# Attention, MLP and routed experts on one core: column-group gate, a new hand-written order, one looped overflow body

## The chip, the core and the metric

The kernel runs on one core of one Trainium2 chip. The metric is device time in microseconds (us): the median of several executions of the whole program. Engines are named as in the profile: PE is the matrix engine (PEld is its loading of weights), DVE the vector engine, ACT the scalar engine, POOL the general engine, SP the engine that issues most DMAs.

## The reference, cut to what matters

```python
# attention: 4 batches x 8 heads, 576 tokens, head_dim 64; heads 0-3 a window of 32 keys,
# heads 4-7 every 4th of the last 128 keys
scores = where(mask, q @ k.T / 8, -1e9)
x = softmax(scores) @ v                      # -> x of 2304 tokens x 512
# block MLP
h = x @ w_in                                 # 512 -> 2048
x = (h * cos(h)) @ w_out                     # 2048 -> 512
# router and experts: 8 experts, two per token
logits = x @ w_gate
noisy = logits + log1p(exp(x @ w_noise)) * noise
top2, their softmax weights
out[t] += weight * (relu(x[t] @ w1[e]) @ w2[e])   # 512 -> 1024 -> 512, for both experts e of t
```

## The kernel before

Three stages follow one another on PE and overlap on the other engines. **Attention** runs in 16 units `u`, each a pair of heads: `a_loadqk` and `a_loadv` (DMA), `a_scores` (PE), `a_exp` (DVE maximum L489, ACT exponentials L509 in many small instructions), `a_norm` (DVE sum and reciprocal, tile `sm`, L520 and L521), and `a_part(u, 0..2)`: transposes (`mt`, L534) and products with the values (`mo`, L554), copied out to `xraw`. `x_split(blk, c)` (L594 on ACT, L595 on DVE) turns `xraw` into the high and low parts `xhl` of the next stage.

**The MLP** runs over 6 blocks of 384 tokens, each in 16 steps `f` of 128 hidden columns, 96 steps in all. In a step PE does `g1` (L607, 12 matmuls into `ph`) and, two steps behind, `g2` (L632, 9 matmuls into `acc`). `post` turns `ph` into `g`: ACT L614, DVE `r` L615, ACT sine and square L617 and L618, DVE `r` again L619, ACT L622, POOL L623. Block 0's 16 steps also bring in the weights: eight pairs `j`, each in four parts `k`. `w_load(j, k)` and for pair 7 `w_piece(7, 0..7)` (half as wide) are DMAs; `w_bits` is three DVE operations (L332, L333, L334, tiles `bits` and `cut`); `w_parts` is an ACT copy (L340) and a POOL subtraction (L341) that leave the two halves in `wm`. Later blocks find all weights in place.

**The router** follows each block: `r_rows` (scaled rows `x1`, written out), `r_trans` (PE transposes `mx` L667, DVE copy `x1t` L668), `r_gate` (fp32 matmuls `mg` L675 against `wgn`, the 8 gate and 8 noise columns; DVE copy `lg` L678, `az` L681), `r_exp`, `r_top`, `r_top2`, `r_pick`, `r_rank`, `r_send`. They are done beside steps of the next block; the last block's router (`LAST`) stands among the first expert's matmuls. **The experts** (`pe` L888, `ye` L923, scatter L936) fill the second half, for up to CAP = 608 tokens of an expert. An overflow test (L1087 to L1093) and `tc.If(over > CAP)` (L1095) stand at the end; with this input no expert exceeds CAP, so its body, eight loops with code of their own, is jumped over.

The order is written by hand. Each engine runs its instructions in the order in which the program calls the functions, and waits at its own head only. `OPENING` is the sequence before and around the first step (`Q4` = `a_loadqk(4)`, `W01` = `w_load(0, 1)`, `B10` = `w_bits(1, 0)`, `P` = `w_parts`, `S`, `E`, `N`, `T`, `A` = the parts of attention, `X` = `x_split`, `G` = pieces of `g1`). `BESIDE` has lines `step:place names`: what is called beside that step, at place -1 before its `g1`, at 0, 1, 2 after pieces of `g2`; for example `8:1 a_loadqk(7) w_bits(5,1) w_parts(5,0) a_exp(6) a_norm(6) w_parts(5,1) w_piece(7,0) w_bits(5,2)`. The DMAs of SP share 8 semaphores, so at most 8 are under way and an issue that has to wait holds all later ones.

Of the kernel before, what the change touches and what calls it, by code (L numbers as in the profile page):

```python
# [102 lines left out]
13:2 w_bits(7,4) w_parts(7,4) w_piece(7,7) w_bits(7,5) w_parts(7,5)
14:0 a_part(7,1)
14:1 w_bits(7,6) w_parts(7,6)
14:2 w_bits(7,7) a_part(7,2) w_parts(7,7)
15:-1 x_split(1,2)
15:0 x_split(1,3)
16:0 a_loadv(8)
# [1069 lines left out]
```

## Time and profile before

| | |
|---|---|
| median of 3 runs | 1045.11 us (1044.08 to 1047.26) |
| the profiled execution's own time | 1044.4 us |
| its span, first to last instruction | 1042.7 us |
| mean granted PE clock over the span | 0.976 |
| PE, PEld, DVE, ACT, POOL busy | 994.9, 878.4, 513.4, 472.4, 353.9 us |
| chain that ended last, by engine | PE 68%, DVE 13%, ACT 8%, POOL 3% |

The granted clock is PE's own, as a share of its full 2.4 GHz; 0.50 is the level of 1.2 GHz. Busy shares are averages over the whole span. The table of stretches (busy time of each engine, granted clock, in each) shows where PE is not busy; the timeline of one engine shows in square brackets how long it was idle ahead of an instruction and which instruction let it go; the chain of waits follows the work that ended last back from step to step, so its times are those that count.

### The profile page before, as it was taken

The page shows a single profiled execution, that of the slowest core. Times are in us where ns is not written, and L with a number is a line of the kernel's source. Part 1 is how long each engine was busy: PE and PEld are TensorE (multiplying, and loading weights), DVE is VectorE, ACT ScalarE, POOL GpSimd, SP SyncE. Part 2 cuts the span into 40 slices and gives each one's busy share as a digit, 9 for nine tenths or more (in the row PEclk, how much of TensorE's full clock was granted, in tenths as well). Part 3 has the DMA queues.
Part 4 walks back from the last instruction along what each step waited for, and adds up shares of the span by engine and source line. Part 5 has one row for each costly group of instructions (what it writes and reads, how often), then busy time and mean ns, then how long its engine had stood idle before and what let it go on. Part 6 is the DMA issues. An engine that isn't in the chain of part 4 may idle for free.

```text
span 1042.7 us, 15952 instructions
## 1 busy us (share of the span) xinstructions
PE 994.9 (95%) x6047; PEld 878.4 (84%) x6047; DVE 513.4 (49%) x1096; ACT 472.4 (45%) x1019; POOL 353.9 (34%) x495
## 2 busy tenths in 40 slices
PE   9788899999999999999999989999999999999995
PEld 7677778888888889989988888899898979898984
DVE  7777755535644453453566444554453535353321
ACT  7677665545656555455465223333241414242210
POOL 5455533343253342142153221441313232322211
PEclk9798889999999999999999999999999999999998
DMA  9972032233221100000324324653434244441201
GB/s 241 349 243 80 21 76 66 90 89 90 79 51 40 48 1 1 31 1 1 112 74 135 122 43 151 225 168 118 149 123 151 72 160 135 155 148 51 69 21 51
DMA packets 71334, 105.13 MB, mean 101 GB/s; under 512 B 31475, under 2 KB 45043, under 8 KB 71248
## 3 DMA queue, kind: packets, MB, share of 16 engines
q1 hardware_dynamic: 61264, 76.34, 23.3%
q0 software_dynamic: 9984, 27.68, 8.6%
q8 instruction: 49, 0.80, 0.4%
q14 instruction: 37, 0.30, 0.1%
HBM read 85.42 MB, written 19.59 MB: 101 GB/s over the span
## 4 chain that ended last, share of the span: by engine, by line
PE 68%; DVE 13%; ACT 8%; issue 4%; POOL 3%; DMA 2%; SPq 1%; DVEq 0%; ACTq 0%; POOLq 0%
PE ye L923 21%; PE pe L888 20%; PE ph L607 11%; PE acc L632 9%; PE mgx L872 2%; DVE r L615 1%; DVE bits L333 1%; DVE bits L332 1%; PE mg L675 1%; ACT r L617 1%; DVE r L619 1%; ACT r L618 1%; PE sc L476 1%; POOL tab L760 1%; DVE cut L334 1%
## 5 line engine op out<-in xcount | busy, mean ns | idle before, releaser
L607 PE MATMUL ph<-xhl,wm 128*128 128x384 f32 x1152 | 230.6, 349 | 8.2 <-DVE r L619 4.3
L632 PE MATMUL acc<-wm,g 128*128 128x512 f32 x864 | 230.9, 405 | 5.8 <-POOL g L623 3.3
L923 PE MATMUL ye<-we,h 128*128 128x512 f32 (+1 forms) x960 | 230.0, 396 | 0.0
L607 PEld LDWEIGHTS ph<-xhl,wm 128*128 128x128 f32 x1152 | 209.8, 195 | 17.6 <-DVE r L619 5.9
L923 PEld LDWEIGHTS ye<-we,h 128*128 128x128 f32 (+1 forms) x960 | 172.9, 183 | 43.0
L632 PEld LDWEIGHTS acc<-wm,g 128*128 128x128 f32 x864 | 161.2, 192 | 35.7 <-POOL g L623 5.6
L623 POOL TENSOR_TENSOR g<-r,g 128x384 fp32r<-128x384 f32 x96 | 97.1, 1013 | 220.1 <-ACT g L622 219.5
L888 PE MATMUL pe<-xga,we 128*128 128x352 f32 x768 | 128.2, 326 | 1.0 <-ACT xga L874 0.6
L888 PEld LDWEIGHTS pe<-xga,we 128*128 128x128 f32 x768 | 125.0, 188 | 1.7 <-ACT xga L874 0.8
L890 ACT ACTIVATE h<-pe 128x352 fp32r<-128x352 f32 (+1 forms) x128 | 54.2, 424 | 131.2 <-PE pe L888 131.2
L891 DVE SCALAR_TENSOR_TENSOR h<-pe,h 128x352 fp32r<-128x352 f32 (+1 forms) x128 | 60.7, 475 | 98.4 <-ACT h L890 97.7
L936 POOL DMA_INDIRECT out<-old,tir x35 | 35.2, 1007 | 211.8 <-DVE old L934 206.7
L615 DVE SCALAR_TENSOR_TENSOR r<-r,ph 128x384 f32<-128x384 int32 x96 | 53.0, 552 | 104.5 <-ACT r L614 104.5
L802 DVE TENSOR_TENSOR we<-wraw,we 128x512 fp32r<-128x512 f32 x128 | 93.0, 734 | 11.0 <-ACT we L801 7.9
L888 PE MATMUL pe<-xgb,we 128*128 128x256 f32 x768 | 94.1, 284 | 3.0 <-DVE xgb L875 1.5
L888 PEld LDWEIGHTS pe<-xgb,we 128*128 128x128 f32 x768 | 93.0, 192 | 3.8 <-ACT xgb L874 1.9
L619 DVE SCALAR_TENSOR_TENSOR r<-r,ph 128x384 f32<-128x384 f32 x96 | 52.8, 550 | 84.5 <-ACT r L618 84.5
L934 DVE SCALAR_TENSOR_TENSOR old<-ye,wts,old 128x512 f32<-128x512 f32 (+1 forms) x35 | 26.3, 750 | 133.4 <-PE ye L923 133.4
L622 ACT ACTIVATE g<-r 128x384 fp32r<-128x384 f32 x96 | 50.2, 523 | 68.5 <-DVE r L619 55.0
L801 ACT ACTIVATE we<-wraw 128x512 fp32r<-128x512 f32 x128 | 78.6, 623 | 0.0
L617 ACT ACTIVATE r<-r 128x384 f32<-128x384 f32 x96 | 50.2, 523 | 55.9 <-DVE r L615 55.5
L614 ACT ACTIVATE r<-ph 128x384 int32<-128x384 f32 x96 | 46.6, 486 | 58.2 <-PE ph L607 51.6
(175 smaller groups left out, 993.1 us busy)
## 6 DMA issues: line engine op xcount, KB each, us to landing
wraw<-in_we SPq DMA_DIRECT2D x64, 512.0 KB, 5.8
raw<-in_wm SPq DMA_DIRECT2D x28, 512.0 KB, 9.3
vts<-in_v SPq DMA_DIRECT2D x13, 384.0 KB, 4.2
x1d<-x SPq DMA_DIRECT2D x18, 256.0 KB, 2.4
out<-zt SPq DMA_DIRECT2D x18, 256.0 KB, 3.7
...
```

Of the source, the lines that this page charges most:

```text
L607: nc.tensor.matmul(ph, w[:, a, o:o + P], XHL[blk, c][:, x, :], start=(c == 0 and n == 0), stop=(c == 3 and n == 2))
L615: nc.vector.scalar_tensor_tensor(r, n, -TWO_PI, ph, op0=ALU.mult, op1=ALU.add)
L617: nc.scalar.activation(r, r, AF.Sin, scale=0.5)
L619: nc.vector.scalar_tensor_tensor(r, r, 0.5, ph, op0=ALU.subtract, op1=ALU.mult)
L623: nc.gpsimd.tensor_tensor(g[:, 1, :], r, g[:, 0, :].bitcast(F32), op=ALU.subtract)
L632: nc.tensor.matmul(ACC[blk][t], g[:, a, t * P:(t + 1) * P], w[:, x, 1024 + j * DM:1024 + (j + 1) * DM], start=(f == 0 and n == 0), stop=(f ...
L801: nc.scalar.activation(t[:, 0, fs], raw, AF.Copy)
L802: eng.tensor_tensor(t[:, 1, fs], raw, t[:, 0, fs].bitcast(F32), op=ALU.subtract)
L888: nc.tensor.matmul(ph[:, :n], w[:, a, o:o + P], x[:, b, c, :], start=(c == 0 and i == 0), stop=(c == 3 and i == 2))
L890: nc.scalar.activation(h[:, 0, f, :], ph[:, :n], AF.Relu)
L891: nc.vector.scalar_tensor_tensor(h[:, 1, f, :], ph[:, :n], 0.0, h[:, 0, f, :].bitcast(F32), op0=ALU.max, op1=ALU.subtract)
L923: nc.tensor.matmul(acc, h[:, a, f, o:o + n], w[:, b, (f % 4) * DM:(f % 4 + 1) * DM], start=(f == 0 and i == 0), stop=(f == 7 and i == 2))
```

## The change

**Gate.** `wgn` becomes 128x4x32, of which a DMA fills 16 columns each and POOL zeroes the rest. In `r_gate` the sides of the matmul are swapped: `wgn[:, c]` (32 columns) is loaded as weights, the 128 tokens of `x1t` stream, and the four chunks `c` of the contraction go to four groups of 32 output partitions of one bank. One DVE copy takes all 384 columns to `lp`. A new function `r_logits` transposes `lp` in three pieces on PE (`ml`), and one DVE reduction adds the four groups into `lg`; `az` follows as before. `r_logits` stands at `20:0`, `36:0`, `52:0`, `68:0`, `84:0`, after the first `acc` of the step behind the gate's, and for `LAST` after `m_g1(0, 0, 2)`, with `r_exp` behind it.

**Order.** `OPENING` and the lines of `BESIDE` for steps 0 to 16 are rewritten. `w_parts` is split in `w_hi` (ACT) and `w_lo` (POOL), `a_part` in `a_tr` (transposes) and `a_o` (products), and these pieces stand apart. What each computes stays.

**Overflow.** The eight loops become one body inside two nested loops; its branch is the same, `over > CAP`. The test has one DVE operation fewer.

```diff
 OPENING = (
-    "S0 S1 E0 N0 Q4 E1 W01 S2 W02 T00 T01 N1 E2 S3 T02 T10a N2 A00 T11 A01 W10 E3 W11 T12 T20a A10a T21a "
-    "A11a N3 B00 T22a X0p A20a W03 B01 T30a V4 P00 A21a X1 T32a W20 X2p S4 P01 T31a G00 "
-    "B10 G10 W23 G11 W12 W21 E4 B11 A30a A31a X3 P10 P11 G01 G02 G12 W13 W22"
+    "W01 S0 S1 W02 E0 N0 S2 W03 E1 T00 Q4 T01 T02 E2 N1 N2 S3 T10a A00 W10 E3 T11 T12 A01 T21a T20a T22a "
+    "A10a N3 B00 A11a B01 W20 W23 X1 T31a A20a P00 X0p P01 T32a A21a T30a S4 G10 G11 W11 E4 W12 B10 W13 "
+    "X2p A30a A31a B11 X3 W22 P10 P11 G00 G01 V4 G12 W21 G02"
 )
 BESIDE = """
-4:1 w_parts(3,0) w_load(4,3) a_scores(5)
-4:2 w_bits(3,1)
-5:-1 a_exp(5) w_parts(3,1) w_load(5,0) a_norm(5) w_load(5,1) w_bits(3,2)
+4:0 a_scores(5) w_hi(2,3) w_load(5,0) w_lo(2,3) w_bits(3,0)
+4:1 w_hi(3,0) w_lo(3,0) a_loadv(5)
+4:2 w_bits(3,1) a_loadqk(6)
+5:-1 w_bits(3,2) a_exp(5) w_hi(3,1) w_load(5,1) w_lo(3,1)
+5:0 a_norm(5)
...
-8:1 a_loadqk(7) w_bits(5,1) w_parts(5,0) a_exp(6) a_norm(6) w_parts(5,1) w_piece(7,0) w_bits(5,2)
+8:0 w_hi(4,3) a_loadv(6) a_scores(6) w_lo(4,3) w_bits(5,0)
+8:1 a_exp(6) w_hi(5,0) w_bits(5,1) w_piece(7,2) a_loadqk(7) w_lo(5,0) a_norm(6) w_bits(5,2)
...
-11:1 a_exp(7) w_bits(7,0) w_parts(6,3) w_bits(7,1) w_parts(7,0) w_parts(7,1)
+11:1 w_bits(7,0) w_hi(6,3) a_exp(7) w_hi(7,0) w_lo(6,3) w_lo(7,0) w_bits(7,1) w_hi(7,1) w_lo(7,1)
...
 19:2 r_gate(0) a_loadqk(9)
-20:0 a_norm(8)
+20:0 a_norm(8) r_logits(0)
 20:1 r_exp(0)
...
+    def w_hi(j, k):
+        nc.scalar.activation(WM[j][:, 0, w_fs(j, k)], CUT[j, k].bitcast(F32), AF.Copy)
+
+    def w_lo(j, k):
         fs = w_fs(j, k)
         raw = CUT.pop((j, k)).bitcast(F32)
-        nc.scalar.activation(WM[j][:, 0, fs], raw, AF.Copy)
         nc.gpsimd.tensor_tensor(WM[j][:, 1, fs], raw, WM[j][:, 0, fs].bitcast(F32), op=ALU.subtract)
...
-    wgn = cpool.tile([P, 4, 2 * NE], F32, name="wgn")
+    wgn = cpool.tile([P, 4, 32], F32, name="wgn")
...
+        G.memset(wgn, 0.0)
...
-        nc.sync.dma_start(wgn, wg)
+        nc.sync.dma_start(wgn[:, :, :2 * NE], wg)
...
-                nc.tensor.matmul(mid[:, t * 2 * NE:(t + 1) * 2 * NE], RT[blk][t][:, c, :], wgn[:, c, :],
-                                 start=(c == 0), stop=(c == 3))
-        lg = small.tile([P, NTB, 2 * NE], F32, tag="lg", name=f"lg{blk}")
-        nc.vector.tensor_copy(lg, mid[:, :NTB * 2 * NE].rearrange("p (t e) -> p t e", t=NTB))
+                nc.tensor.matmul(mid[32 * c:32 * c + 32, t * P:(t + 1) * P], wgn[:, c, :], RT[blk][t][:, c, :],
+                                 start=True, stop=True)
+        lp = tpool.tile([P, DM], F32, tag="t2", name=f"lp{blk}")[:, :TB]
+        nc.vector.tensor_copy(lp, mid[:, :TB])
+        RT[blk] = lp
+
+    def r_logits(blk):
+        lp = RT[blk]
+        mid = r_bank(f"ml{blk}", blk)
+        for t in range(NTB):
+            nc.tensor.transpose(mid[:, t * P:(t + 1) * P], lp[:, t * P:(t + 1) * P], ident)
+        lg = small.tile([P, NTB, 32], F32, tag="lg", name=f"lg{blk}")
+        nc.vector.tensor_reduce(lg, mid[:, :TB].rearrange("p (t c e) -> p t e c", c=4, e=32), axis=AX.X, op=ALU.add)
...
     with tc.If(over > CAP):
-        for e in range(NE):
-            nt = nc.values_load(nti[0:1, e:e + 1], min_val=NTILE, max_val=NTILE + -(-(NT - CAP) // P))
-            with tc.For_i(NTILE, nt, 1) as i:
+        nt = nc.values_load(nti[0:1, 1:2], min_val=NTILE, max_val=NTILE + -(-(NT - CAP) // P))
+        with tc.For_i(NTILE, nt, 1) as i:
+            with tc.For_i(0, NE, 1) as e:
```

What the order looks like on the engines, at three places. First SP's queue behind the last DMA of the constants (`tab`), before; `raw0` holds pair 0 of the weights, and `kts` and `qts` belong to unit 4, `vts` too:

```order
L428 DMA tab_81<-padt_191 128x300
L276 DMA kts_83<-in_kT 128x576
L279 DMA qts_85<-in_qT 64x9x64 x2
L307 DMA raw0_104<-in_wm 128x1024 x2
L307 DMA raw1_379<-in_wm 128x1024 x2
L307 DMA raw0_104<-in_wm 128x1024
L284 DMA vts_84<-in_v 64x128
L285 DMA vts_84<-in_v 96x8x128
```

and the same place after:

```order
L445 DMA tab_81<-padt_191 128x300
L317 DMA raw0_104<-in_wm 128x1024 x3
L286 DMA kts_83<-in_kT 128x576
L289 DMA qts_85<-in_qT 64x9x64 x2
L317 DMA raw1_364<-in_wm 128x1024
L317 DMA raw2_453<-in_wm 128x1024 x2
```

The three loads of pair 0 stand ahead of unit 4's keys and queries, and the values of unit 4 further behind.

Second, DVE at steps 12 and 13, before:

```order
L521 RECIPROCAL sm7_1372<-sm7_1372 128x9
L615 SCALAR_TENSOR_TENSOR r0_12_1426<-r0_12_1426,ph0_12_1408 128x384
L332 TENSOR_SCALAR bits7_2_1435<-piece7_2_1280 128x256
L333 SCALAR_TENSOR_TENSOR bits7_2_1435<-piece7_2_1280,bits7_2_1435 128x256
L334 SCALAR_TENSOR_TENSOR cut7_2_1434<-piece7_2_1280,bits7_2_1435 128x256
L332 TENSOR_SCALAR bits7_3_1442<-piece7_3_1432 128x256
L333 SCALAR_TENSOR_TENSOR bits7_3_1442<-piece7_3_1432,bits7_3_1442 128x256
L334 SCALAR_TENSOR_TENSOR cut7_3_1441<-piece7_3_1432,bits7_3_1442 128x256
L619 SCALAR_TENSOR_TENSOR r0_12_1426<-r0_12_1426,ph0_12_1408 128x384
L595 TENSOR_TENSOR xhl1_1_1455<-xraw_82,xhl1_1_1455 128x384
L615 SCALAR_TENSOR_TENSOR r0_13_1484<-r0_13_1484,ph0_13_1469 128x384
L619 SCALAR_TENSOR_TENSOR r0_13_1484<-r0_13_1484,ph0_13_1469 128x384
```

and after:

```order
L342 TENSOR_SCALAR bits7_2_1430<-piece7_2_1161 128x256
L343 SCALAR_TENSOR_TENSOR bits7_2_1430<-piece7_2_1161,bits7_2_1430 128x256
L344 SCALAR_TENSOR_TENSOR cut7_2_1429<-piece7_2_1161,bits7_2_1430 128x256
L628 SCALAR_TENSOR_TENSOR r0_12_1434<-r0_12_1434,ph0_12_1411 128x384
L342 TENSOR_SCALAR bits7_3_1447<-piece7_3_1440 128x256
L343 SCALAR_TENSOR_TENSOR bits7_3_1447<-piece7_3_1440,bits7_3_1447 128x256
L344 SCALAR_TENSOR_TENSOR cut7_3_1446<-piece7_3_1440,bits7_3_1447 128x256
L632 SCALAR_TENSOR_TENSOR r0_12_1434<-r0_12_1434,ph0_12_1411 128x384
L608 TENSOR_TENSOR xhl1_1_1456<-xraw_82,xhl1_1_1456 128x384
L628 SCALAR_TENSOR_TENSOR r0_13_1488<-r0_13_1488,ph0_13_1473 128x384
L342 TENSOR_SCALAR bits7_4_1495<-piece7_4_1051 128x256
L343 SCALAR_TENSOR_TENSOR bits7_4_1495<-piece7_4_1051,bits7_4_1495 128x256
```

One piece of weight work has moved ahead of the first `r` of step 12, and between the two `r` of step 13, where nothing stood, there is one now.

Third, PE at the gate of block 0, beside steps 19 and 20, before:

```order
L632 MATMUL acc1_2_1744<-wm0_436,g1_1_1708 128x512 x3
L675 MATMUL mg0_1833<-wgn_187,x1t0_0_1768 128x16 x4
L675 MATMUL mg0_1833<-wgn_187,x1t0_1_1787 128x16 x4
L675 MATMUL mg0_1833<-wgn_187,x1t0_2_1813 128x16 x4
L607 MATMUL ph1_4_1853<-xhl1_0_1253,wm2_707 128x384 x3
L607 MATMUL ph1_4_1853<-xhl1_1_1455,wm2_707 128x384 x3
L607 MATMUL ph1_4_1853<-xhl1_2_1623,wm2_707 128x384 x3
L607 MATMUL ph1_4_1853<-xhl1_3_1632,wm2_707 128x384 x3
L632 MATMUL acc1_0_1742<-wm1_533,g1_2_1778 128x512 x3
L632 MATMUL acc1_1_1743<-wm1_533,g1_2_1778 128x512 x3
```

and after:

```order
L645 MATMUL acc1_2_1745<-wm0_430,g1_1_1709 128x512 x3
L688 MATMUL mg0_1834<-x1t0_0_1769,wgn_187 32x128 x4
L688 MATMUL mg0_1834<-x1t0_1_1788,wgn_187 32x128 x4
L688 MATMUL mg0_1834<-x1t0_2_1814,wgn_187 32x128 x4
L620 MATMUL ph1_4_1852<-xhl1_0_1257,wm2_692 128x384 x3
L620 MATMUL ph1_4_1852<-xhl1_1_1456,wm2_692 128x384 x3
L620 MATMUL ph1_4_1852<-xhl1_2_1629,wm2_692 128x384 x3
L620 MATMUL ph1_4_1852<-xhl1_3_1633,wm2_692 128x384 x3
L645 MATMUL acc1_0_1743<-wm1_544,g1_2_1779 128x512 x3
L698 MATMUL ml0_1878<-ident_131,lp0_1847 128x128 x3
L645 MATMUL acc1_1_1744<-wm1_544,g1_2_1779 128x512 x3
```

The 12 calls of the gate stand where they stood, with weights and stream swapped, and the three transposes `ml` stand in PE's queue 15 matmuls behind them.

## Rows read from the trace of the kernel before

**Rows 1.** The page: busy time and share; the chain that ended last, by engine

```profile
PE 994.9 (95%) x6047; PEld 878.4 (84%) x6047; DVE 513.4 (49%) x1096; ACT 472.4 (45%) x1019; POOL 353.9 (34%) x495
...
PE 68%; DVE 13%; ACT 8%; issue 4%; POOL 3%; DMA 2%; SPq 1%; DVEq 0%; ACTq 0%; POOLq 0%
```

**Rows 2.** Stretches: length, busy us (instructions) per engine, PE clock, DMA share, GB/s

```profile
26.00:52.00 26.00, 19.30 (x125) 17.39 (x127) 18.44 (x31) 16.03 (x45) 12.30 (x13) 0.74 1.06 349
...
40.00:157.00 117.00, 101.24 (x600) 86.08 (x599) 85.07 (x151) 79.73 (x202) 61.66 (x62) 0.87 0.43 128
157.00:1031.00 874.00, 859.26 (x5117) 763.97 (x5115) 400.26 (x881) 366.51 (x703) 272.18 (x386) 1.00 0.28 90
```

**Rows 3.** Timeline of DVE, opening: start, us, operation, [idle before <- releaser]

```profile
27.29 0.69 DVE L332 TENSOR_SCALAR bits<-raw 128x512 uint32<-128x512 uint32 x1 [3.84 <-DMA raw<-in_wm]
```

**Rows 4.** Timeline of PE, opening and first steps

```profile
26.32 1.33 PE L476 MATMUL sc<-kts,qts 128*128 128x96 f32 x10 [0.90 <-DMA qts<-in_qT]
...
33.72 2.61 PE L554 MATMUL mo<-ahat,ahead 96*64 96x64 f32 x40 [3.14 <-ACT s L509]
36.26 4.39 PE L607 MATMUL ph<-xhl,wm 128*128 128x384 f32 x15
43.89 4.21 PE L607 MATMUL ph<-xhl,wm 128*128 128x384 f32 x12 [3.24 <-DVE r L619]
```

**Rows 5.** Timeline of DVE around step 5

```profile
73.13 0.17 DVE L520 TENSOR_SCALAR sm<-sm 128x9 f32<-128x9 f32 x1 [2.89 <-ACT s L509]
...
77.28 0.55 DVE L619 SCALAR_TENSOR_TENSOR r<-r,ph 128x384 f32<-128x384 f32 x1 [1.14 <-ACT r L618]
```

**Rows 6.** Timeline of DVE at step 8

```profile
100.84 0.17 DVE L520 TENSOR_SCALAR sm<-sm 128x9 f32<-128x9 f32 x1 [2.16 <-ACT s L509]
```

**Rows 7.** Timeline of DVE at steps 11 and 12

```profile
126.38 0.42 DVE L334 SCALAR_TENSOR_TENSOR cut<-piece,bits 128x256 uint32<-128x256 uint32 x1 [2.60 <-POOL wm L341]
...
134.28 0.55 DVE L619 SCALAR_TENSOR_TENSOR r<-r,ph 128x384 f32<-128x384 f32 x1 [2.87 <-ACT r L618]
```

**Rows 8.** Chain of waits around block 0's gate: start, us, what

```profile
167.22 0.44 PE mx L667 x4
...
169.05 2.58 PE mg L675 x24
171.63 3.07 PE ph L607 x12
```

**Rows 9.** All of tile mg: ns min/median/max, first and last start, form

```profile
L675 PE MATMUL mg<-wgn,x1t x144: 176/263/263, 168.9 to 573.5; 128*128 128x16 f32 x144
```

**Rows 10.** Timeline of DVE at the same gate

```profile
171.78 0.56 DVE L619 SCALAR_TENSOR_TENSOR r<-r,ph 128x384 f32<-128x384 f32 x1 [3.39 <-ACT r L618]
172.25 0.20 DVE L678 COPY lg<-mg 128x48 f32<-128x48 f32 x1
```

**Rows 11.** Timeline of PE: a run of 20 matmuls in two column groups

```profile
51.65 0.78 PE L554 MATMUL mo<-at,vts 96*64 96x64 f32 x20
52.36 0.53 PE L534 MATMUL mt<-ident,s 128*96 128x128 f32 x3
```

**Rows 12.** Stretches at half clock, columns as in Rows 2

```profile
73.70:80.50 6.80, 6.43 (x19) 5.17 (x20) 5.38 (x10) 5.41 (x10) 5.39 (x6) 0.50 0.33 130
...
172.70:176.10 3.40, 3.40 (x11) 3.12 (x10) 0.79 (x2) 0.94 (x3) 1.00 (x1) 0.50 0.00 0
```

**Rows 13.** Chain of waits, its last piece

```profile
1031.93 0.99 POOL out L936
```

**Rows 14.** Line L1095, the overflow branch: ns min/median/max, first and last start

```profile
L1095 SPq EVENT_SEMAPHORE  x9: 17/17/17, 1036.4 to 1037.0; - x9
...
L1095 PEldq COMPARE_BRANCH  x1: 4925/4925/4925, 1032.9 to 1032.9; - x1
...
L1095 POOLq INC_SWDGE_SEM  x1: 1015/1015/1015, 1037.4 to 1037.4; - x1
```

**Rows 15.** Line L1175, the end of the program

```profile
L1175 POOLq DRAIN  x3: 46/107/3425, 1038.4 to 1042.4; - x3
```

More of the change, by code (lines that the diff above doesn't have):

```diff
@@ L103 @@
[L103 to L109, printed above, removed]
+0:-1 w_load(3,0) w_bits(0,2)
+0:1 w_hi(0,2) w_bits(0,3) w_lo(0,2)
+0:2 w_hi(0,3) w_lo(0,3) a_norm(4)
+1:0 w_bits(1,2)
+1:1 w_hi(1,2) w_bits(1,3) w_lo(1,2)
+1:2 a_loadqk(5)
+2:-1 w_load(3,3)
+2:0 w_bits(2,0) w_load(4,0) a_tr(4,0) a_tr(4,1) w_hi(1,3) w_lo(1,3)
+2:1 w_hi(2,0) w_load(4,1) w_bits(2,1) w_load(4,3)
@@ new lines @@
+6:2 w_bits(4,1)
+7:-1 w_load(5,3)
+7:0 w_bits(4,2) w_load(5,2) w_hi(4,1) a_o(5,0) w_piece(7,4) w_lo(4,1)
+7:1 w_load(6,3) a_tr(5,2) w_hi(4,2) w_lo(4,2)
+7:2 w_piece(7,1)
+8:-1 w_bits(4,3) a_o(5,1)
+8:0 w_hi(4,3) a_loadv(6) a_scores(6) w_lo(4,3) w_bits(5,0)
+8:1 a_exp(6) w_hi(5,0) w_bits(5,1) w_piece(7,2) a_loadqk(7) w_lo(5,0) a_norm(6) w_bits(5,2)
+8:2 w_hi(5,1)
+9:-1 w_lo(5,1)
+9:0 w_load(6,1)
+9:2 a_tr(6,0) a_tr(6,1)
+10:-1 w_bits(5,3)
+10:0 w_hi(5,2) x_split(1,0)
+10:1 w_hi(5,3) w_lo(5,2) a_o(6,0) w_lo(5,3) a_tr(6,2)
@@ L110 @@
+14:-1 w_lo(7,5)
+14:0 a_tr(7,2) w_bits(7,6)
+14:1 w_hi(7,6) w_lo(7,6)
+14:2 w_bits(7,7)
+15:-1 a_o(7,1) w_hi(7,7)
+15:0 x_split(1,2) w_lo(7,7) x_split(1,3)
+16:2 a_loadv(8)
 17:0 x_split(2,0) x_split(2,1)
@@ L136 @@
 31:2 zero_out(10)
-32:0 a_part(10,0)
-32:2 a_part(10,1)
-33:0 a_part(10,2)
+32:0 a_tr(10,0) a_tr(10,1)
+32:2 a_o(10,0) a_tr(10,2)
+33:0 a_o(10,1)
 33:2 r_rows(1) a_loadv(11)
@@ L193 @@
 67:2 r_gate(3)
+68:0 r_logits(3)
 68:1 r_exp(3)
@@ L1003 @@
     m_g1(0, 0, 2)
+    r_logits(LAST)
+    r_exp(LAST)
     r_top(LAST)
@@ L1093 @@
-    nc.vector.tensor_copy(nti[:, NE:], mxc)
-    over = nc.values_load(nti[0:1, NE:NE + 1], min_val=0, max_val=NT)
+    mxc = small.tile([P, 2], F32, tag="mxc", name="mxc", bufs=1)
+    nc.vector.tensor_reduce(mxc[:, 0:1], cnt, axis=AX.X, op=ALU.max)
+    nti = small.tile([P, 2], I32, tag="nti", name="nti", bufs=1)
+    nc.vector.tensor_scalar(mxc[:, 1:2], mxc[:, 0:1], float(CAP), None, op0=ALU.max)
+    nc.vector.tensor_scalar(mxc[:, 1:2], mxc[:, 1:2], 1.0 / P, (63.5 - CAP) / P + NTILE, op0=ALU.mult, op1=ALU.add)
@@ L1111 @@
                 nc.gpsimd.indirect_dma_start(out=od, out_offset=None, in_=out,
                                              in_offset=bass.IndirectOffsetOnAxis(ap=idc[:, :1], axis=0))
-                wt = [ring.tile([P, 2, 2048], F32, tag="ring", name=f"gw{e}_{j}") for j in range(2)]
+                wt = [ring.tile([P, 2, 2048], F32, tag="ring", name=f"gw_{j}") for j in range(2)]
                 for j in range(2):
-                    nc.sync.dma_start(wt[j], we[2 * e + j])
-                mid = psum.tile([P, 512], F32, tag="mid", name=f"gm{e}", bufs=2)
+                    nc.sync.dma_start(wt[j], we[bass.ds(2 * e + j, 1)].rearrange("o p k f -> p (o k) f"))
@@ L1128 @@
                     nc.scalar.activation(h[:, f, :], ph[:, :P], AF.Relu)
-                acc = bank(f"gy{e}")
+                acc = bank("gy")
                 for f in range(8):
```

151 lines of the change are left out of this document (64 added, 87 removed).

## The prediction, made before the changed kernel ran

> **What bounds the kernel now.** I read the page first. PE is busy for 95% of the span and holds 68% of the chain that ended last; DVE has 13% of it, ACT 8% [rows 1]. Such shares are averages, so the table of stretches comes next: from 157 to 1031 us PE is busy 859.26 of 874.00 us at a granted clock of 1.00, but from 40 to 157 us only 101.24 of 117.00, at a clock of 0.87, and between 26 and 52 us 19.30 of 26.00, at 0.74 [rows 2]. Behind 157 us a change can win only by giving PE less to do, or at the very end. Before 157 us PE waits for others, and there an order can win something. Those 117 us are the 16 steps of block 0, 7.3 us a step. No engine is full in them: DVE has 85.07 us of work, ACT 79.73, POOL 61.66 [rows 2]. What bounds them is a ring: PE's `ph` goes through ACT, DVE, ACT, DVE, ACT and POOL back to PE, while the same engines cut up weights and do attention. An idle DVE there, with an `[idle before <- releaser]`, is where the ring stands still.
>
> **The change part by part**, summed against the profiled execution, 1044.4 us, 1.7 us more than its span. It lies 0.7 us under the median, 1045.11, and the three runs differ by 3 us among themselves; I carry the same sum over to the median.
>
> *Opening.* SP now issues W01, W02 and W03 ahead of unit 4's keys and queries. DVE idles 3.84 us for W01 [rows 3]; PE waits for those queries until 26.32, so W01, which arrives 0.9 us or so behind them, is the next load [rows 3, 4]. At 349 GB/s [rows 2] a 512 KB load takes 1.5 us and unit 4's 576 KB take 1.7. So W01 comes some 1.7 us sooner (up to 2.7, with the issue of the queries gone from ahead of it) and the queries 2.5 to 4.5 us later: two or three loads. The weights' gain isn't the start's gain. The first large `ph` run starts at 36.26, behind a run of `mo` that waited 3.14 us for ACT's exponentials [rows 4], and those need the scores of unit 4's neighbours in PE's own queue. I take +0.5 us for the start of step 0, with -1 (W01 counts) and +3.5 (the queries count) as ends. The wider `wgn` is one DMA of smaller pieces in the same queue, and a POOL clear; under 0.5 us, within those ends.
>
> *Step 5.* DVE stands 2.89 us at `sm`, waiting for nine exponentials of ACT, with the cuts of part (3,2) (three operations of 0.69 [rows 3], 2.1 us) queued behind [rows 5]. The change puts those three and the first `r` ahead of `sm`, and unit 5's maximum ahead of part (3,0), so that the exponentials start sooner. At most 2.1 us are won, at least nothing: behind it the second `r` still waits 1.14 us for ACT [rows 5], and ACT's exponentials are only moved, not removed. I take 0.8, about a third. *Step 8.* The same wait, 2.16 us [rows 6]; here unit 6's maximum moves ahead of part (5,0) and the exponentials ahead of an ACT copy. 0 to 2.1, and I take 1.2, since ACT itself is let go earlier.
>
> *Steps 11 and 12.* DVE idles 2.60 us because a cut's buffer is still read by POOL's subtraction, which waited for an ACT copy behind unit 7's exponentials; then 2.87 us before the second `r` of step 12, for sine and square [rows 7]. In the new order that ACT copy stands ahead of the exponentials, and one piece of cutting has gone ahead of the first `r`. Of 5.5 us I take a third, 1.85; 0 to 4. *Steps 13 to 15.* Between the two `r` of a step DVE waited about 1.15 us, as at 77.28 [rows 5], for ACT, with the cuts queued behind; now a cut of three half operations stands in the gap of steps 13 and 14. Two gaps are worth 2.3 us at most; I take 1.0. The later loads of pieces 7_3, 7_5, 7_6 and 7_7 wait for buffers, but their cuts stand later too; at nothing, covered by DVE's work ahead of them, and up to 1 us each if that is gone.
>
> Sum of block 0: +0.5 - 0.8 - 1.2 - 1.85 - 1.0 = **-4.35 us**; the ends are -10 and +3.5.
>
> *Gate.* In the chain the 24 instructions of a gate take 2.58 us [rows 8], 0.108 us each, at 144 / 6 = 24 a block [rows 9]. Five of the six lie in the loop, where PE is the bound, so they count in full. After, the stream is 128 columns instead of 16, and four groups of 32 output columns can stand side by side. The nearest row on groups is attention's `mo`: 20 instructions with 64 columns in two groups take 0.71 us to the next operation, 0.036 each [rows 11]. For 128 columns that is twice as much in two groups, 0.071, and 0.036 each if four run abreast: 24 of them take 0.85 to 1.7. Without any overlap they cost what a 128-column transpose does, 0.44 / 4 = 0.11 [rows 8], 2.64. I take 1.3, the middle of the first two, and 0.35 for going into the mode and out, an estimate from `mo`, whose group costs some 0.2 to 0.3 beyond its pace: 1.65. New are three transposes, 3 x 0.11 = 0.33. Net 2.58 - 1.65 - 0.33 = 0.6 us won a block, 5 x 0.6 = **-3.0**; ends: four abreast with nothing for the mode, 2.58 - 0.85 - 0.33 = 1.4 won, or no overlap and the mode's price, 2.64 + 0.35 + 0.33 - 2.58 = 0.74 lost. DVE gets 0.9 us more a block (a 384-column copy and a reduction at 0.5 to 0.6 each instead of 0.20 [rows 10]), beside matmuls. The sixth gate waits in a DVE chain; at nothing.
>
> The Trainium skill, "TensorEngine Tiling (Array Packing)", section Key Properties, says that changing the tiling mode drains the engine, and its section Theoretical Speedup that 32 columns are good for up to 4 times. By the full fourfold the matmuls would take 2.58 / 4 = 0.65 us and each block would win 1.6; no row here shows four groups, and `mo` shows two.
>
> *Clock.* After block 0's gate the granted clock is 0.50 for 3.40 us [rows 12], and at half clock that costs 1.7. The gate's 16-column matmuls had ended 1.1 us ahead of it [rows 8]. A gate of another form may take it away; **-1.2**, ends 0 and -1.7. In block 0 the level falls too, for 6.80 us right after an idle PE [rows 12]; but steps there aren't PE's, so I count nothing.
>
> *The end.* The last scatter is issued at 1031.93 [rows 13]. At the branch PE needs 4.9 us, and POOL goes on only at 1037.4, then 1.0 and 3.4 us of clean-up end the span [rows 14, 15]. With a small body there is little to jump over and so nothing to bring in. What is left is the scatter's own landing, which by the first semaphore events of that line is no later than 1036.4 on SP; from there to 1037.4 are 1.0 us, of which POOL's own few events keep some 0.2. **-0.75**, ends 0 and -0.8.
>
> Sum: -4.35 - 3.0 - 1.2 - 0.75 = -9.3, so 1035.1 for the profiled execution and 1045.11 - 9.3 = 1035.8 for the median; I say **1036**.
>
> **Rivals.** *Four groups run abreast at the pace of one.* Then 6 slots of 0.108 are 0.65 us, each block wins 2.58 - 0.65 - 0.33 = 1.6, and five win 8.0 instead of 3.0: 1031. For it: `mo`'s two groups do cost little. Against: none of its instructions is closer than 0.036 on average. The page named with the gate gives the same.
>
> *Block 0 doesn't follow.* DVE's holes close, but ACT, with 79.73 of 117 us in the same ring, or PE at half clock [rows 2, 12] sets the same end; only gate, clock and tail are won: 1045.11 - 4.95 = 1040. For it: in each of the four places ACT released DVE, or POOL behind ACT [rows 5 to 7], and ACT's work isn't less.
>
> *Groups don't overlap.* The gate loses 0.74 x 5 = 3.7 and the clock stays: 1045.11 - 4.35 - 0.75 + 3.7 = 1043.7, no difference that can be told.
>
> *PE waits for `lp`; slower.* In PE's queue `ml` stands 15 matmuls behind the gate, and `lp` on DVE stands behind the second `r`, which in block 1 came 3.39 us late, at 171.78, since ACT was late [rows 10]. From the end of the gate PE has 12 `ph` and 3 `acc`, some 2.8 us at full clock, before it stands. Before, `lg` ran 0.6 us after the gate ended at 171.63 [rows 8, 10]; a gate that ends 1.0 sooner leaves `lp` done about 2.2 us after it, 0.6 us in time. Were `r` so late at all five gates that PE waits 3 us each, the gate's gain of 3.0 turns into a loss of 12, the clock's is gone as well, and the time is 1045.11 - 5.1 + 12 = 1052. Slower by over 0.3% (3.1 us) begins where the loss at gates passes 8.2 us, a wait of 2.2 us in each. Against: DVE has half its time free there, 400.26 of 874 us busy [rows 2].
>
> *The change doesn't do what it says*: loads that arrive late in the new order of SP's queue, or a branch that takes as long as before, undo what the rest wins: 1044.5.
>
> **How the numbers follow.** My forecast, with its part sizes within 1032 to 1039: 0.45. Four abreast (about 1031): 0.12. Block 0 doesn't follow (1040, from 1039 to 1042.5): 0.19. Groups don't overlap (1043.7): 0.09. Undone (1044.5): 0.07. `lp` or another new wait (1050): 0.08. About 0.3%, 3.1 us, is what a measurement of this kernel can tell from no change; that bound is 1042.0 to 1048.2. Faster: 0.45 + 0.12 + 0.17 = 0.74; within: 0.02 of the hidden gain + 0.09 + 0.07 - 0.01 = 0.17; slower: 0.08 and 0.01 of the undone case = 0.09. For 8 in 10 the range leaves out the slower cases, half of the undone and of the gate's loss, and little below: 1029 to 1043.7.
>
> **What would show it.** In the profile of the changed kernel `mg` should take 1.3 to 1.7 us in the chain and `ml` 0.3 to 0.4, with no idle PE ahead of `ml`; if `mg` stays at 2.6, groups don't overlap, and if PE idles there, DVE's `lp` was late. Between 40 and 157 us PE's clock should stay about 0.87 and that stretch end 4 us sooner, with the holes at `sm` of units 5 and 6 smaller; if they are gone and the stretch is as long, ACT bounds it. The clock at the first gate's end should be 1.00. From the last scatter's issue to the span's end there should be 10 us instead of 10.7. The forecast is wrong if the first `ph` run starts 2 us later than 36.26, since block 0's gains then only pay for that.

## The result, and the profile after

The changed kernel took 1032.41 us (median of 4 runs, 1029.02 to 1035.32) where the kernel before took 1044.76 (4 runs): a ratio of 0.9876, with a 95% interval of 0.9836 to 0.9917. That is 12.3 us won; 1036 was predicted, 9.3 won by its sum, in a range of 1029 to 1043.7. The sign and the range held. The terms behind them did not all hold, and two that were missed by much had opposite signs.

The profiled execution of the changed kernel took 1034.67 us, its span is 1033.0. Its page, with the lines that answer to [rows 1]:

```profile
PE 983.7 (95%) x6065; PEld 864.0 (84%) x6065; DVE 516.5 (50%) x1101; ACT 472.0 (46%) x1019; POOL 353.7 (34%) x496
...
PE 70%; DVE 12%; ACT 8%; POOL 3%; DMA 2%; issue 2%; SPq 1%; DVEq 0%; ACTq 0%; POOLq 0%
```

PE is busy 11 us less (994.9 before), of which the gate alone, put into the kernel before, shows 6 (988.9); what makes the rest isn't shown. DVE is busy 3 us more. The stretches of [rows 2] after the change (length, busy us and instructions of PE, PEld, DVE, ACT, POOL, granted clock, DMA share, GB/s):

```profile
26.00:52.00 26.00, 15.74 (x119) 14.12 (x120) 14.06 (x24) 14.22 (x41) 9.88 (x9) 0.80 1.08 323
40.00:157.00 117.00, 100.13 (x633) 85.06 (x634) 87.24 (x156) 84.48 (x218) 64.32 (x64) 0.93 0.43 133
157.00:1025.00 868.00, 853.26 (x5136) 754.41 (x5134) 404.14 (x887) 365.83 (x703) 272.12 (x386) 0.99 0.28 90
```

From 26 to 52 us PE does less than before (15.74 us against 19.30), so the opening got worse; from 40 to 157 us 633 matmuls go through where 600 did, so block 0 got better.

The first DVE `r` of each step (L615 before, L628 after) has a record in every one of the 96 steps and makes a good mark, counted here from step 0. What lies between such marks, and at the end, in the traces of the kernel before (two executions, the second from the last experiment), of the changed kernel (two, the second from the run called again) and of the two kernels with one part of the change:

| stretch | before | before, 2nd | after | after, 2nd | gate alone | order alone |
|---|---|---|---|---|---|---|
| start to step 0 | 40.69 | 40.41 | 46.30 | 45.73 | 46.81 | 41.97 |
| steps 0 to 4 | 23.26 | 23.26 | 22.39 | 22.40 | 23.26 | 22.40 |
| steps 4 to 8 | 27.09 | 27.10 | 26.69 | 26.52 | 27.09 | 25.40 |
| steps 8 to 9 | 12.25 | 12.26 | 11.02 | 11.01 | 12.25 | 11.00 |
| steps 9 to 16 | 48.77 | 48.15 | 44.90 | 44.86 | 47.98 | 47.28 |
| steps 19 to 21, gate of block 0 | 16.08 | 15.21 | 14.16 | 14.16 | 14.16 | 15.22 |
| steps 35 to 39, gate of block 1 and what follows | 26.18 | 27.55 | 29.01 | 28.96 | 27.71 | 27.69 |
| of these, step 38 to 39 | 6.52 | 6.53 | 9.32 | 9.28 | 8.02 | 6.53 |
| steps 48 to 52, gate of block 2 | 24.56 | 24.56 | 22.79 | 22.78 | 22.82 | 24.51 |
| steps 62 to 68, gate of block 3 | 29.11 | 29.15 | 27.41 | 27.41 | 27.40 | 29.15 |
| steps 78 to 84, gate of block 4 | 29.11 | 29.11 | 27.42 | 27.42 | 27.44 | 29.11 |
| last row update to the end | 11.81 | 11.73 | 8.02 | 8.02 | 12.23 | 11.82 |

Most rows answer to one part of the change. The opening does not: it is late with the gate alone, but hardly with the order alone. It and the rows of block 1 are those in which the changed kernel is slower. At the mark of step 16, behind the opening and block 0 together, the changed kernel stands at 151.30 and 150.53 us, the kernel before at 152.05 and 151.19: of the forecast 4.35 us between nothing and 1.5 is won there.

**The gate.** All instructions of tile `mg`, the line of [rows 9] (ns min/median/max, first and last start, form):

```profile
L688 PEld LDWEIGHTS mg<-x1t,wgn x144: 106/110/111, 169.2 to 565.6; 128*32 128x32 f32 x144
L688 PE MATMUL mg<-x1t,wgn x144: 272/273/298, 169.2 to 565.7; 128*32 128x128 f32 x144
```

and PE's timeline at block 0's gate, which answers to [rows 8] (start, us, operation, count):

```profile
169.19 0.86 PE L688 MATMUL mg<-x1t,wgn 128*32 128x128 f32 x24
169.98 2.35 PE L620 MATMUL ph<-xhl,wm 128*128 128x384 f32 x12
172.17 0.86 PE L645 MATMUL acc<-wm,g 128*128 128x512 f32 x3
173.06 0.55 PE L698 MATMUL ml<-ident,lp 128*128 128x128 f32 x3
173.37 1.64 PE L645 MATMUL acc<-wm,g 128*128 128x512 f32 x6
```

One matmul lasts 273 ns as before (263), but 24 of them take 169.98 - 169.19 = 0.79 us instead of 2.58: 0.033 us each. The transposes take 0.31 (173.37 - 173.06). DVE's `lp` stands where the prediction put it, and PE's waits say what that cost (engine, line, releaser: us in total, times, longest):

```profile
PEld ml L698 <- DVE lp L691: 0.9, 2, 0.5
```

**The end.** The lines that answer to [rows 14], now line L1117:

```profile
L1117 SPq EVENT_SEMAPHORE  x4: 17/17/17, 1027.7 to 1028.0; - x4
...
L1117 POOLq EVENT_SEMAPHORE  x2: 17/30/43, 1027.5 to 1027.6; - x2
...
L1117 POOLq COMPARE_BRANCH  x1: 54/54/54, 1027.0 to 1027.0; - x1
L1117 PEldq COMPARE_BRANCH  x1: 227/227/227, 1027.0 to 1027.0; - x1
...
L1117 SPq COMPARE_BRANCH  x1: 45/45/45, 1027.2 to 1027.2; - x1
L1117 POOLq INC_SWDGE_SEM  x1: 1024/1024/1024, 1027.7 to 1027.7; - x1
```

and the last scatter, from the chain of waits (start, us, what):

```profile
1025.98 0.99 POOL out L958
```

PE is through the branch in 0.2 us instead of 4.9, and POOL begins its clean-up at 1027.7, 1.7 us after the last scatter was issued at 1025.98; before, it was 5.5 us.

### The profile page after: what moved, and what is told of

Read it like the earlier page. It is cut to its first block, busy times and chain, and to the rows that moved or that the text cites. A ratio compares the mean times of both kernels' runs of the same rounds, so it can differ in the third digit from the quotient of the medians.

```text
span 1033.0 us, 16001 instructions
## 1 busy us (share of the span) xinstructions
PE 983.7 (95%) x6065; PEld 864.0 (84%) x6065; DVE 516.5 (50%) x1101; ACT 472.0 (46%) x1019; POOL 353.7 (34%) x496
## 4 chain that ended last, share of the span: by engine, by line
PE 70%; DVE 12%; ACT 8%; POOL 3%; DMA 2%; issue 2%; SPq 1%; DVEq 0%; ACTq 0%; POOLq 0%
PE ye L945 21%; PE pe L910 20%; PE ph L620 11%; PE acc L645 11%; PE sc L493 2%; PE mgx L894 1%; DVE r L628 1%; DVE r L632 1%; POOL tab L782 1%; DMA qts<-in_qT 1%; ACT r L630 1%; ACT r L631 1%; ACT s L526 1%; DVE bits L343 1%; DMA ahead<-in_v 1%
## 5 line engine op out<-in xcount | busy, mean ns | idle before, releaser
L620 PE MATMUL ph<-xhl,wm 128*128 128x384 f32 x1152 | 225.5, 344 | 7.6 <-DVE r L632 3.2
L620 PEld LDWEIGHTS ph<-xhl,wm 128*128 128x128 f32 x1152 | 206.1, 192 | 17.0 <-DVE r L632 3.7
L628 DVE SCALAR_TENSOR_TENSOR r<-r,ph 128x384 f32<-128x384 int32 x96 | 53.0, 552 | 105.7 <-ACT r L627 105.6
```

Of the source, the lines that this page charges most:

```text
L620: nc.tensor.matmul(ph, w[:, a, o:o + P], XHL[blk, c][:, x, :], start=(c == 0 and n == 0), stop=(c == 3 and n == 2))
L628: nc.vector.scalar_tensor_tensor(r, n, -TWO_PI, ph, op0=ALU.mult, op1=ALU.add)
```

## The experiments

Each kernel was timed beside the kernel before on the same chip; that one's median was 1049.27 (33 runs) beside the first four, 1047.23 (11 runs) beside the next four, 1046.37 (11 runs) and 1048.93 (13 runs) beside the rest.

**One part alone: gate, order, loop, open.** The kernel before with the gate's lines of the diff, with both tables, with the overflow body, and with OPENING alone.

> The kernel before with the gate's change alone (column groups, lp, ml). Theory, from the trace of the changed kernel, where a gate's 24 matmuls took 0.79 us instead of 2.6 and the transposes 0.30: each of the five gates in the loop wins 1.5 to 1.75 us, so 1044.8 - 8 = 1037. Rival one, also from that trace: behind block 1's gate PE arrives sooner at a wait for DVE and the clock falls, which gives 2.8 back: 1039.6. Rival two, the prediction on record: 0.6 a block, 3.0 and 1.2 for the clock: 1040.6.

Measured: 1043.69, ratio 0.9943 (0.9920 to 0.9965), 5.6 us won. In its trace the gates of blocks 2 to 4 win 1.67 to 1.75 us each, as the theory said, and the stretch of block 1's gate gives nothing (27.71). That trace is of the slowest of its ten executions (1049.97), and its step 0 comes 6.1 us late: the median's gain is read from the times, not from this span.

> The kernel before with the two tables of order alone (OPENING and BESIDE), gate and overflow as before. Theory, from the marks of each step in the changed kernel's trace: the first step starts 5.6 us later, since unit 4's queries land behind three loads of weights, and block 0 wins 6.35, so nothing is left: 1044. Rival one: 2.4 of the 5.6 belong to that one execution, in which all loads after 20 us landed late: 1041.6. Rival two, the prediction on record: 4.35 won, 1040.4.

Measured: 1045.95, ratio 0.9966 (0.9946 to 0.9985), 3.3 to 3.6 us won. The forecast's 4.35 lies inside that interval (1.6 to 5.7), the theory of nothing left doesn't. In its trace step 0 starts only 1.3 us later and steps 0 to 16 win 4.7 to 5.3.

> The kernel before with the overflow body as one loop, all else as before. Theory, from the changed kernel's trace, where the span ended 7.3 us after the last row update instead of 11.1: no code is brought in at the branch and the scatter's landing doesn't count, 3.8 us won: 1041.0. Rival, the prediction on record: the scatter's landing takes the place of the fetch, 0.75 won: 1044.0.

```diff
-        for e in range(NE):
-            nt = nc.values_load(nti[0:1, e:e + 1], ...)
-            with tc.For_i(NTILE, nt, 1) as i:
+        nt = nc.values_load(nti[0:1, 1:2], ...)
+        with tc.For_i(NTILE, nt, 1) as i:
+            with tc.For_i(0, NE, 1) as e:
```

Measured: 1044.38, ratio 0.9949 (0.9931 to 0.9967), 4.9 to 5.4 us won, within its interval the 3.8 that the trace shows: from the last row update to the end 8.01 us instead of 11.81 and 11.73. The branch line of that trace, L1093, has the same short jump:

```profile
L1093 PEldq COMPARE_BRANCH  x1: 373/373/373, 1038.0 to 1038.0; - x1
...
L1093 POOLq INC_SWDGE_SEM  x1: 1017/1017/1017, 1038.7 to 1038.7; - x1
```

> The kernel before with the new OPENING alone, BESIDE as before. Theory: the queries of unit 4 land 4 to 7 us later, PE stands at their scores with the first step's matmuls queued behind, and the first step starts 3 to 5.6 us later; block 0's holes are DVE's waits for ACT, which move with it, so the loss stays: 1048 to 1050. Rival: block 0 is paced by the loads and takes the delay up: 1045. The prediction on record took 0.5 us: 1045.3.

Measured: 1049.64, ratio 1.0001 (0.9983 to 1.0018): no difference. PE does stand longer at the queries, as its timeline shows (in brackets the idle time ahead and what ended it),

```profile
30.56 1.33 PE L476 MATMUL sc<-kts,qts 128*128 128x96 f32 x10 [2.67 <-DMA qts<-in_qT]
```

2.67 us instead of 0.90 [rows 4], and yet the first `r` comes at 40.62, where it came at 40.69. The theory falls; the 0.5 us on record is within what this kernel shows, in a trace of the fastest of its twelve executions (1044.49). The three kernels that share no line add up: 0.9943 x 0.9966 x 0.9949 = 0.986, and the whole change measured 0.9876.

**The whole again, and three variants of it.**

> The changed kernel once more, as a measure for its variants on the same chip. If the parts simply add (gate 5.6, order 3.5 and loop 3.8 won, as the kernels with one part each showed), it is 12.9 us faster than the kernel before, about 1036 where that one is at 1049. If the first step's late start in its first trace (5.6 us) belongs to the kernel, its new trace starts near 46 us again; if it was the loads of that one execution, near 41 to 42.

Measured: 1034.28, ratio 0.9875 (0.9854 to 0.9896), 12.9 us won. Step 0 starts at 45.73 again, late.

> The changed kernel, but the four chunks of the contraction are accumulated in one group of 32 output partitions: weights and stream stay swapped, no groups stand side by side, and the transposes take 32 partitions. Theory: it is the groups that overlap, so the 24 matmuls go back to about 0.11 us each, 2.6 us a gate, and each of the five gates loses 1.7 to 1.8: 8 to 9 us slower than the changed kernel, apart from what block 1 gives back. Rival: the short weights (32 columns instead of 128) are what pays: the gate stays under 1.2 us and the time within 2 us of the changed kernel.

```diff
-                nc.tensor.matmul(mid[32 * c:32 * c + 32, t * P:(t + 1) * P], wgn[:, c, :], RT[blk][t][:, c, :],
-                                 start=True, stop=True)
+                nc.tensor.matmul(mid[:32, t * P:(t + 1) * P], wgn[:, c, :], RT[blk][t][:, c, :],
+                                 start=(c == 0), stop=(c == 3))
```

Measured: 1042.05, 7.8 us slower than the changed kernel beside it. PE's timeline at the same gate:

```profile
169.45 2.81 PE L688 MATMUL mg<-x1t,wgn 128*32 128x128 f32 x24
172.19 2.35 PE L620 MATMUL ph<-xhl,wm 128*128 128x384 f32 x12
```

The same 24 matmuls with the same short weights, in one group of outputs instead of four, take 172.19 - 169.45 = 2.74 us instead of 0.79. Neither the swap nor the shorter weights pay; four groups side by side do, at 2.74 / 0.79 = 3.5 times the pace, whatever going into that mode costs included. The edit also brings back the accumulation over the four chunks, but that isn't what costs: the transposes, which accumulate nothing, take 0.11 us each too [rows 8].

> The changed kernel with two pieces of block 1's router later in the order of DVE: r_top2(1) from 36:2 to 37:2, r_pick(1) from 37:2 to 38:2. Theory: behind block 1's gate PE runs into a wait at step 38 that ends with DVE's small operations, its idle time grows from 0.35 to 1.32 us there, and the clock at 0.50 from 278 to 284 us costs another 2.8; without them 2 to 4 us are won and the clock stays at 1.00 there. Rival: the wait is for ACT's copy of the transposes whatever stands on DVE, the clock falls all the same, and nothing changes.

```diff
-36:2 r_top(1) r_top2(1) zero_out(11)
-37:2 a_o(11,0) a_tr(11,2) r_pick(1)
-38:2 a_loadv(12) zero_out(13)
+36:2 r_top(1) zero_out(11)
+37:2 a_o(11,0) a_tr(11,2) r_top2(1)
+38:2 a_loadv(12) zero_out(13) r_pick(1)
```

Measured: 1029.90 (1027.96 to 1031.86), 4.4 us faster than the changed kernel beside it. The changed kernel at step 38, PE's timeline and two stretches:

```profile
274.93 0.89 PE L571 MATMUL mo<-at,vts 96*64 96x32 f32 x20 [1.32 <-DVE m L741]
275.75 1.35 PE L493 MATMUL sc<-kts,qts 128*128 128x96 f32 x10
277.91 1.99 PE L493 MATMUL sc<-kts,qts 128*128 128x96 f32 x8 [0.81 <-DVE xraw L588]
```

```profile
276.00:280.00 4.00, 3.19 (x19) 3.05 (x19) 2.95 (x13) 1.04 (x2) 0.93 (x1) 0.64 0.53 168
280.00:284.00 4.00, 4.00 (x12) 3.42 (x12) 1.51 (x3) 0.52 (x1) 1.67 (x3) 0.51 0.74 180
```

the kernel before at the same place:

```profile
276.81 0.89 PE L554 MATMUL mo<-at,vts 96*64 96x32 f32 x20 [0.35 <-DVE m L719]
277.63 1.35 PE L476 MATMUL sc<-kts,qts 128*128 128x96 f32 x10
279.80 1.10 PE L476 MATMUL sc<-kts,qts 128*128 128x96 f32 x8 [0.81 <-DVE xraw L571]
```

```profile
278.00:282.00 4.00, 3.19 (x23) 2.84 (x23) 3.81 (x13) 1.05 (x2) 0.99 (x1) 1.00 0.58 172
```

and the kernel with the two pieces moved:

```profile
272.68 0.88 PE L571 MATMUL mo<-at,vts 96*64 96x32 f32 x20 [0.37 <-DVE den L729]
273.49 1.35 PE L493 MATMUL sc<-kts,qts 128*128 128x96 f32 x10
275.18 1.10 PE L493 MATMUL sc<-kts,qts 128*128 128x96 f32 x8 [0.33 <-DVE xraw L588]
```

```profile
276.00:280.00 4.00, 4.00 (x23) 3.70 (x23) 3.81 (x19) 0.63 (x2) 2.83 (x3) 1.00 0.81 227
280.00:284.00 4.00, 4.00 (x30) 3.46 (x29) 0.94 (x5) 3.94 (x5) 0.00 (x0) 1.00 0.61 214
```

In the changed kernel PE idles 1.32 and 0.81 us and the clock stands near 0.5 for the next 6 us; the same 8 matmuls take 1.99 us instead of 1.10. The kernel before has the wait of 0.81 as well, but 0.35 ahead of it, and its clock stays at 1.00. With DVE's small operations out of the way the waits are 0.37 and 0.33, the clock stays at 1.00, and steps 35 to 39 take 24.78 us instead of 29.01. The theory holds, and these 4.2 us are all but 0.2 of the variant's gain. Not all of it is the new wait: step 38 to 39 goes back from 9.32 to 6.53 us, the kernel before's, which is 2.8; the other 1.4 come in the three steps ahead, which are now shorter than they were before the change.

> The changed kernel with unit 4's keys and queries issued behind W01 alone instead of behind W01, W02 and W03. Theory: PE stands 2.4 to 6.1 us at these queries with the first step's matmuls behind, so they arrive 2.5 us sooner and the first step starts 1 to 2.5 us sooner, which the end keeps: 1 to 2.5 us won. Rival: W02 and W03 then come later by 1.7 us, and DVE, which cuts them, starts the first step no sooner: nothing.

Measured: 1032.72 (1031.98 to 1034.01), 1.6 us below the changed kernel (1033.32 to 1034.76); the two groups of four runs overlap a little. In its trace the queries are there at 29.9 us instead of 32.7 and step 0 starts at 42.52 instead of 45.73. Of these 3.2 us the whole execution keeps 1.0 (1032.34 and 1033.32 us). It points to the theory without settling it, since executions of one kernel differ by as much.

**The opening, and all improvements together.**

> The changed kernel, but the DMA of the gate's weights into the widened tile (now 64-byte pieces) is issued at step 14 instead of in the opening. Theory: in the seven traces so far the last constants (tab) land at 22.9 to 24.9 us without the wider tile and at 24.3 to 27.0 with it, so this DMA holds the loads behind it up by 1 to 2 us; without it W01 and unit 4's queries land that much sooner, the first step starts 1 to 2 us sooner, and the time is 1 to 2 us lower than the changed kernel's. Rival: the loads' lateness is chance from one execution to the next, and nothing changes.

Measured: 1033.73 (1027.47 to 1036.97), ratio 0.9860 (0.9833 to 0.9886), no different from the changed kernel's 0.9875. In its trace, of the slowest of its six executions, `tab` lands at 26.55, later still, with that DMA out of the way. Nothing supports this theory.

> The changed kernel with the OPENING of before; gate, steps and overflow body as changed. Theory: the new OPENING costs the first step nothing to 3 us (the queries behind three loads) and is repaid in the steps, which find their weights sooner; without it the time is 0 to 2 us higher than the changed kernel's. Rival: it is all cost, as PE's wait of 2 to 6 us for the queries suggests, and the time is 2 to 4 us lower.

Measured: 1032.74 (1030.38 to 1033.23), ratio 0.9855 (0.9833 to 0.9877) where the changed kernel had 0.9875 and 0.9876: the new OPENING brings nothing that can be measured, in line with the kernel that had it alone. In its trace step 0 comes at 43.17.

> The changed kernel with three edits: r_top2(1) and r_pick(1) later (4.4 us measured), unit 4's queries behind W01 alone (1.6 measured), the gate's weights issued at step 14. If they add, 1034.3 - 4.4 - 1.6 - 1 to 2 = 1026 to 1027 where the changed kernel is at 1034; if the last two win the same wait, 1028.

Measured: 1028.44 (1027.70 to 1031.17), ratio 0.9831 (0.9809 to 0.9853): faster than either kernel of the change, but not faster than the variant with r_top2 and r_pick alone, 0.9832 (0.9812 to 0.9852). If the edits of the opening add to it, it is less than these intervals can tell. Its trace repeats the gain at step 38: 6.50 us to step 39.

> The kernel before once more, unchanged, for a second trace of it. Theory: the arrival of the opening's loads differs by some us from one execution to the next whatever the kernel, so that tab, which landed at 23.08 us in the first trace, lands elsewhere between 23 and 27 and the first step's r moves from 40.69 with it; the tail from the last row update to the end stays at 11 to 12 us, and steps 53 to 94 stay at their places relative to each other within 0.1. Rival: the first trace is typical, tab lands within 0.5 us of 23.08, and the later start of the changed kernel (44.7 to 46.3) is its own.

Measured: 1048.59, ratio 1.0007 (0.9985 to 1.0030). `tab` lands at 22.33, 0.75 us sooner and not later, and step 0's `r` is at 40.41. The start of the first trace was typical of the kernel before, as the rival had it; the five traces with its gate lie between 40.41 and 42.56, those of the changed kernel at 45.73 and 46.30. The tail stays (11.73 us), and steps 53 to 91 keep their places within 0.1, but not those up to 94: step 93 to 94 took 6.91 us instead of 4.48. Others moved as well: steps 35 to 39 took 27.55 us instead of 26.18 and steps 39 to 48 52.92 instead of 51.47, of which PE's timeline shows

```profile
304.89 1.13 PE L476 MATMUL sc<-kts,qts 128*128 128x96 f32 x8 [1.21 <-issue]
```

a wait that the first trace doesn't have. The traces of gate, order and OPENING alone have it too, 1.05 to 1.14 us long; in the last DVE's copy to `xraw` ends it. Here it is the first trace that stands apart.

## Why the prediction was right, and where it was not

*Opening, +0.5 predicted.* For the order of the loads alone this was near: OPENING alone gave -0.07 us at step 0, both tables +1.3. In the changed kernel step 0 comes 5.0 to 5.6 us later, outside the bound of 3.5. Its PE shows where:

```profile
33.40 2.42 PE L493 MATMUL sc<-kts,qts 128*128 128x96 f32 x10 [6.06 <-DMA qts<-in_qT]
...
37.50 1.61 PE L620 MATMUL ph<-xhl,wm 128*128 128x384 f32 x6
...
43.09 2.36 PE L620 MATMUL ph<-xhl,wm 128*128 128x384 f32 x11 [0.58 <-POOL xhl L608]
```

PE stands 6.06 us at the queries, and as it has idled, the same ten matmuls take 2.42 us at half clock that took 1.33 [rows 4]. Of the large `ph` runs, the one of 15 matmuls stood at 36.26 [rows 4]; now none of more than 6 starts before 41 us. So the sign by which the prediction called itself wrong, a start 2 us later that block 0's gains only pay for, is what happened.

The step that failed is the bound of +3.5, and with it the gate's part in the opening, "under 0.5 us, within those ends". What share each has isn't shown. With the old tile `tab` landed at 22.3 to 24.9 us in five traces and step 0 stood at 40.4 to 42.6; with the wide one it was 24.2 to 27.0 in nine traces and 42.5 to 47.0. But two traces with the old OPENING and the wide tile have 43.17 (the changed kernel with the OPENING of before) and 46.81 (the gate alone), and in the second SP came to the issue of `wgn` at 18.18 us, where the kernel before did at 15.10: half of its 6.1 us stand ahead of that DMA. Its being in the queue isn't shown to be the reason: in the two traces without it there `tab` landed no sooner, at 26.55 and, with all improvements together, at 25.89. Whether it is the clearing on POOL, the other places of the tiles behind it, or chance in nine against five traces, stays open; it wasn't tried.

*Block 0, -4.85 predicted behind the opening.* Steps 0 to 16 won 4.7 to 5.3 us (order alone) and 5.8 to 6.6 (the changed kernel), against either trace of the kernel before. The prediction's end of -10 for the opening and block 0 is a wrong sum of its own ends, -1 - 2.1 - 2.1 - 4 - 2.3 = -11.5; nothing measured came near it. By places: step 8 won 1.2, as predicted. Steps 4 to 8, step 5's 0.8, won 0.4 and 0.6 in the changed kernel, but 1.7 with order alone and in all six variants of the changed kernel, so 1.7 is the rule. Steps 9 to 16, the terms 1.85 and 1.0, won 3.3 to 3.9, or 0.9 to 1.5 with order alone; of the six variants three lie at either. The first four steps won 0.86, which the prediction didn't have. DVE's timeline shows what the change did to the holes (those of [rows 5] and [rows 7], with the idle time in brackets):

```profile
78.74 0.55 DVE L628 SCALAR_TENSOR_TENSOR r<-r,ph 128x384 f32<-128x384 int32 x1 [1.50 <-ACT r L627]
79.21 0.49 DVE L537 TENSOR_SCALAR sm<-sm 128x9 f32<-128x9 f32 x1
...
129.59 0.17 DVE L537 TENSOR_SCALAR sm<-sm 128x9 f32<-128x9 f32 x1 [1.78 <-ACT s L526]
...
135.99 0.56 DVE L632 SCALAR_TENSOR_TENSOR r<-r,ph 128x384 f32<-128x384 f32 x1 [2.87 <-ACT r L631]
```

The wait of 2.89 us at `sm` is gone, and in its place DVE waits 1.50 at the first `r` ahead of it, for another copy of ACT; that of 2.60 for POOL became 1.78 for ACT; the wait of 2.87 for sine and square at step 12 is still 2.87. Holes closed by a third to a half, since ACT is what DVE then waits for. Taking a third of each hole was of the right kind and mostly too low. By the steps the rival "block 0 doesn't follow" is out; its gain went to the opening.

*Gate, -3.0 predicted.* The sign and the mechanism were right and the size was wrong in two places. The 24 matmuls were put at 1.65 us and took 0.79: of the price for the mode, 0.35, little or nothing is there, and the four groups run faster than the 0.036 us of `mo` that served as the bound (0.033). So a gate wins 1.67 to 1.78 where PE is the bound (blocks 2 to 4), and the rival "four abreast", with 1.6, was right about the gates. The Trainium skill, "TensorEngine Tiling (Array Packing)", section Theoretical Speedup, has up to 4 times for 32 columns; the trace agrees, with 3.5. The Trainium skill, "TensorEngine Tiling (Array Packing)", section Key Properties, says that a change of the tiling mode drains the engine. If it does here, going in and out costs at most 0.14 us, an estimate: the 0.79 us from the gate's first matmul to the first `ph` behind it, less 2.58 / 4 = 0.65. On the other side, the rival "PE waits for `lp`" had the right idea and the wrong place. `ml` waited 0.9 us in two gates together. The new wait is two steps on in block 1, where DVE has 0.9 us more to do and PE comes sooner: 1.32 us instead of 0.35 and 0.19, and behind it step 38 to 39, at half clock, takes 9.3 us instead of 6.5, 2.8 more, in both traces of the changed kernel. The whole stretch from step 35 to 39 lost 2.8 against the first trace of before and 1.4 against the second. The five gates together won 3.3 to 4.7 us by the marks, measured alone 5.6 (3.7 to 8.4).

*Clock behind the first gate, -1.2 predicted.* The stretch at 0.50 is gone, but it was no fixed part of the kernel before: in its second trace, with the old gate, the clock is 1.00 from 150 to 178 us and steps 19 to 21 take 15.21 us instead of 16.08. Order alone and the overflow body alone have 15.22 and 15.20, OPENING alone 16.09. Nor is a cost of the fallen clock left at step 21: steps 16 to 21 together are 31.19 us with it and 31.13 without, in the two traces of before. After the change they take 30.22, so the gate of block 0 wins some 1 us. The step that failed is reading one execution's fallen clock as the gate's.

*The end, -0.75 predicted.* It won 3.8, and the failed step is "what is left is the scatter's own landing". The first semaphore events at 1036.4 [rows 14] were read as the scatter's landing; they were SP's own return from the jump, as the branches of before show:

```profile
L1095 POOLq EVENT_SEMAPHORE  x5: 17/43/43, 1037.0 to 1037.3; - x5
...
L1095 POOLq COMPARE_BRANCH  x1: 58/58/58, 1032.9 to 1032.9; - x1
...
L1095 SPq COMPARE_BRANCH  x1: 50/50/50, 1033.2 to 1033.2; - x1
```

SP's first event came 3.2 us behind its branch and POOL's 4.1; over the small body both come after 0.5. After the change POOL is past the branch 1.7 us after the scatter's issue, and the clean-up of 3.4 us behind it takes as long as ever. All of PE's 4.9 us at the branch but 0.2 were the jump over the large body. From the last scatter's issue to the span's end there are 7.0 us, where the prediction's sign was 10.

In sum: +0.5 came out as +5.0 to 5.6, -4.85 as -5.8 to -6.6, -3.0 as -3.3 to -4.7, -1.2 as nothing that the change can be shown to have won, -0.75 as -3.8. The profiled executions lie 9.7 us apart (1044.4 and 1034.67), the medians 12.3 and, again, 12.9. The predicted time was near by luck as much as by its mechanisms, because errors of opposite sign met, the opening on one side, the end and block 0 on the other.
